# Fused cross-covariance attention and gated FFN on one core: the short chunk of v first in each batch, and the early loads in another order

## The chip, the cores and the metric

The kernel runs on one core of a Trainium2 chip. The metric is the device time of one execution in microseconds (us); smaller is better. Kernels that are compared ran in alternating rounds on the same chip. In the profile lines, PE is TensorE's products, PEld its weight loads, DVE VectorE, ACT ScalarE, POOL GpSimd and SPq SyncE's queue; a timeline line gives start and length in us, and in brackets the idle time before it and what ended it.

## The reference, cut to what matters

```python
# four batches, N = 6016 tokens, C = 256 channels, d_ff = 1536
qn = q / (norm(q, axis=1) + 1e-06);  kn = k / (norm(k, axis=1) + 1e-06)   # over the tokens
s = kn.transpose(0, 2, 1) @ qn / tau                  # 256 x 256 for each batch
a = softmax(s)
x = (v @ a).reshape(B * N, C)
out = (sigmoid(x @ w_gate) * (x @ w_val)) @ w_out
```

The matrix a of a batch needs all of that batch's q and k. After that, v can be streamed through in pieces. The kernel never forms x: it multiplies a into the weights first (G = a·w_gate, H = a·w_val), so that each piece of v needs only v·G, v·H and the output product.

## The kernel before

A batch has 47 tiles of 128 tokens, in chunks of four tiles and one "short" chunk of three. While TensorE streams the chunks of one batch, it also forms the scores of the next batch, and VectorE the squares for its norms. The work is laid out in slots: twelve slots a chunk, and slot f computes one slice of 128 of d_ff.

```python
groups = [(t, min(TPC, NT - t)) for t in range(0, NT, TPC)]     # TPC = 4, NT = 47: the short one is last
...
psg = pool("psg", 2, space=PSUM)     # gate products, two buffers
psv = pool("psv", 2, space=PSUM)     # value products, two buffers
...
def glu(b, ci, f):                   # one slot: 4 matmuls as wide as the chunk (512 or 384)
    ...
    nc.scalar.activation(out=g_sb[:, :n], in_=ps_gate[:, :n], func=ACT.Sigmoid)
    nc.vector.tensor_tensor(
        out=hts[b, ci][:, f, :n], in0=ps_val[:, :n], in1=g_sb[:, :n], op=ALU.mult)    # hT
...
for ci in range(NCH):                # the main loop, inside "for b in range(B)"
    for f in range(FC):              # FC = 12
        glu(b, ci, f)
        flush()                      # copies finished output rows out of PSUM, stores a finished chunk
        if prev is not None and not block:
            out_mms(*prev, f * TPC, (f + 1) * TPC)    # four output products of the chunk before
        for fn, a in side.get((ci, f), ()):           # loads, transposes, scores, squares
            fn(*a)
        if (b, ci) == (0, 0) and f < len(gh_order) - 5:
            gh(0, 5 + f, pso, "o")                    # the last 7 of batch 0's 12 pieces of G and H
```

The first two v chunks of batch 0 are transposed on TensorE, the others by a DMA that the SyncE queue issues. That queue works in order, and the store of a finished chunk stands in it ahead of the transpose of a later one.

## Time and profile before

| | before |
|---|---|
| median of the first three runs | 829.01 us (828.88 to 829.31) |
| the first profiled execution | 830.27 us, with a span of 828.2 us from first to last instruction |
| TensorE busy | 807.9 us, 98% of that span |
| VectorE, ScalarE busy | 590.2 us (71%), 392.2 us (47%) |

The prediction quotes the lines of this profile.

### The profile page before, as it was taken

Reading aid. Unit: us, or ns where it says so; the run is one execution under the profiler, and the core shown is the slowest. Engines: PE = TensorE matmul, PEld = TensorE weight load, DVE = VectorE, ACT = ScalarE, POOL = GpSimd, SP = SyncE. Lnnn points to the kernel's source line nnn. Section 1 sums busy time; section 2 is a strip of 40 time slices with the busy share of each in tenths; the row PEclk is TensorE's granted clock in tenths of the full one; section 3 lists DMA queues with packets and bytes.
Section 4 is the critical chain, followed back from the end, with each engine's and each line's share of the span. In section 5 each row is a group of like instructions: output and inputs, shape, how many; then the busy total and the mean of one; then the engine's idle time right before and its main releaser. Section 6 shows DMA issues by size and latency. Waiting matters only on the chain.

```text
span 828.2 us, 13621 instructions
## 1 busy us (share of the span) xinstructions
PE 807.9 (98%) x5122; PEld 499.1 (60%) x5134; DVE 590.2 (71%) x1025; ACT 392.2 (47%) x644; POOL 78.9 (10%) x151
## 2 busy tenths in 40 slices
PE   4799999999999999999999999999999999999998
PEld 2456666665665666665576666666566566666666
DVE  5777777887667777778767777777766666666665
ACT  3754444446644444445654444444655444444442
POOL 4432100002201100000221010000000000000000
PEclk9999999999999999999999999999999999999999
DMA  9999823226746443223875452223322323322211
GB/s 214 206 200 195 126 52 89 55 58 133 158 85 124 96 85 60 57 51 83 157 141 123 81 108 60 51 60 78 64 58 63 75 52 84 61 58 68 47 36 71
DMA packets 77874, 77.17 MB, mean 93 GB/s; under 512 B 50672, under 2 KB 55792, under 8 KB 77808
## 3 DMA queue, kind: packets, MB, share of 16 engines
q0 software_dynamic: 22768, 38.81, 28.5%
q1 hardware_dynamic: 54752, 36.91, 17.6%
q8 instruction: 40, 0.66, 0.3%
q10 hardware_dynamic: 288, 0.59, 0.2%
q14 instruction: 26, 0.21, 0.1%
HBM read 78.64 MB, written 24.64 MB: 125 GB/s over the span
## 4 chain that ended last, share of the span: by engine, by line
PE 92%; DMA 6%; DVE 1%; issue 0%; POOL 0%; ACT 0%; POOLq 0%
PE ps_o L88 29%; PE ps_gate L88 29%; PE ps_val L88 29%; PE ps_s L88 4%; DMA k_sb<-in_k_dram 3%; PE ps_gh L88 2%; DMA vT<-v_sb 2%; DMA w_gate<-in_moe_w_gate_dram 1%; DVE hT L434 0%; DVE sq L184 0%; PE ps_end L88 0%; ACT g_sb L433 0%; POOL q_sb L98 0%; PE ps_n L88 0%; POOL k_sb L98 0%
## 5 line engine op out<-in xcount | busy, mean ns | idle before, releaser
L434 DVE TENSOR_TENSOR hT<-ps_val,g_sb 128x512 bf16<-128x512 f32 (+1 forms) x576 | 391.0, 679 | 205.7 <-ACT g_sb L433 200.8
L433 ACT ACTIVATE g_sb<-ps_gate 128x512 bf16<-128x512 f32 (+1 forms) x576 | 338.2, 588 | 386.8 <-PE ps_gate L88 380.5
L88 PE MATMUL ps_gate<-vT,gh_G 128*128 128x512 bf16 (+1 forms) x1152 | 337.5, 375 | 0.7 <-DMA vT<-v_sb 0.5
L88 PE MATMUL ps_val<-vT,gh_H 128*128 128x512 bf16 (+1 forms) x1152 | 337.5, 375 | 0.3
L88 PE MATMUL ps_o<-w_out_sb,hT 128*128 128x256 bf16 x2244 | 324.9, 273 | 0.0
L88 PEld LDWEIGHTS <-hT 128*128 128x128 bf16 x2268 | 221.0, 98 | 124.7
L88 PEld LDWEIGHTS <-gh_H 128*128 128x128 bf16 x1152 | 112.7, 98 | 131.7 <-issue 1.0
L88 PEld LDWEIGHTS <-gh_G 128*128 128x128 bf16 x1152 | 112.4, 98 | 38.3 <-DMA vT<-v_sb 0.8
L460 DVE COPY out_sb<-ps_o 128x256 f32<-128x256 f32 x187 | 77.4, 414 | 12.6 <-PE ps_o L88 12.6
L88 PE MATMUL ps_s<-k_sb,q_sb 128*128 128x256 bf16 x376 | 71.2, 293 | 14.6 <-DMA k_sb<-in_k_dram 7.6
L108 POOL DMA_DIRECT2D v_sb<-in_v_dram x48 | 25.5, 532 | 601.3 <-DMA vT<-v_sb 452.0
L88 PEld LDWEIGHTS <-q_sb 128*128 128x128 bf16 x376 | 39.2, 105 | 23.7 <-issue 9.6
L223 DVE TENSOR_TENSOR acc<-acc,sq 128x1024 bf16<-128x1024 bf16 (+1 forms) x66 | 44.2, 669 | 0.0
L184 DVE TENSOR_TENSOR sq<-q_sb 128x1024 bf16<-128x1024 bf16 (+2 forms) x42 | 28.0, 666 | 1.2 <-DMA q_sb<-in_q_dram 1.1
L98 POOL DMA_DIRECT2D q_sb<-in_q_dram x44 | 24.2, 549 | 38.5 <-PE ps_s L88 12.4
L98 POOL DMA_DIRECT2D k_sb<-in_k_dram x44 | 24.0, 544 | 14.5 <-DMA k_sb<-in_k_dram 7.7
L184 DVE TENSOR_TENSOR sq<-k_sb 128x1024 bf16<-128x1024 bf16 (+2 forms) x34 | 22.4, 658 | 0.2 <-DMA k_sb<-in_k_dram 0.2
L182 ACT ACTIVATE sq<-k_sb 128x1024 bf16<-128x1024 bf16 (+1 forms) x11 | 10.7, 1010 | 12.0 <-DMA k_sb<-in_k_dram 8.9
L88 PEld LDWEIGHTS <-e_sb 128*128 128x128 bf16 x112 | 10.2, 98 | 6.0 <-issue 1.0
L88 PE MATMUL ps_gh<-w_val,e_sb 128*128 128x512 bf16 x45 | 13.5, 379 | 0.2
L88 PE MATMUL ps_gh<-w_gate,e_sb 128*128 128x512 bf16 x41 | 12.7, 379 | 1.0 <-DMA w_gate<-in_moe_w_gate_dram 0.8
L433 ACT ACT_TABLE_LOAD x6 | 7.7, 1283 | 9.0 <-PE ps_gate L88 9.0
(69 smaller groups left out, 123.2 us busy)
## 6 DMA issues: line engine op xcount, KB each, us to landing
out_dram<-out_sb SPq DMA_DIRECT2D x44, 512.0 KB, 2.9
v_sb<-in_v_dram POOLq DMA_DIRECT2D x44, 256.0 KB, 3.9
q_sb<-in_q_dram POOLq DMA_DIRECT2D x35, 256.0 KB, 6.5
k_sb<-in_k_dram POOLq DMA_DIRECT2D x35, 256.0 KB, 7.7
q_sb<-in_q_dram POOLq DMA_DIRECT2D x4, 512.0 KB, 11.5
k_sb<-in_k_dram POOLq DMA_DIRECT2D x4, 512.0 KB, 13.4
out_dram<-out_sb SPq DMA_DIRECT2D x3, 384.0 KB, 3.0
w_gate<-in_moe_w_gate_dram POOLq DMA_DIRECT2D x3, 256.0 KB, 8.0
```

Source lines behind the costliest of these rows:

```text
L88: nc.tensor.matmul(out, lhsT=lhsT, rhs=rhs, start=start, stop=stop, **kw)
L98: nc.gpsimd.dma_start(out=tl[:, :nt, :], in_=rows(src, b)[:, t0 : t0 + nt, :])
L108: nc.gpsimd.dma_start(out=v_sb[:, :nt, :], in_=rows(v, b)[:, t0 : t0 + nt, :])
L182: nc.scalar.activation(out=sq[:, :nt, :], in_=src[:, :nt, :], func=ACT.Square)
L184: engine.tensor_tensor(out=sq[:, :nt, :], in0=src[:, :nt, :], in1=src[:, :nt, :], op=ALU.mult)
L223: nc.vector.tensor_tensor(out=acc[:, :nt, :], in0=acc[:, :nt, :], in1=st[b]["sq", w][:, :nt, :], op=ALU.add)
L433: nc.scalar.activation(out=g_sb[:, :n], in_=ps_gate[:, :n], func=ACT.Sigmoid)
L434: nc.vector.tensor_tensor(out=hts[b, ci][:, f, :n], in0=ps_val[:, :n], in1=g_sb[:, :n], op=ALU.mult)
L460: nc.vector.tensor_copy(out=out_sb[:, s, :], in_=ps)
```

## The change

It has three parts. The short chunk comes first in each batch, so that the first piece of v is smaller and the stream can start earlier. During batch 0, the loads of the next batch's q and k are put eight slots later in program order (12 instead of 20 slots before use). And the output weights are loaded ahead of the third v chunk.

```diff
+    short = NT - (NCH - 1) * TPC
+    chunks = [(0, short)] + [(short + t * TPC, TPC) for t in range(NCH - 1)]
 ...
     def load_v(b, ci):
-        t0, nt = groups[ci]
+        t0, nt = chunks[ci]
 ... (the same in transpose_v, glu, out_mms, flush, last_rows and the last loop)
-            if lb < B:
-                at(ci * FC + 0, load_v, lb, lci)
             if (b, ci) == (0, 0):
                 at(0, load_w_out)
+            if lb < B:
+                at(ci * FC + (1 if (b, ci) == (0, 0) else 0), load_v, lb, lci)
 ...
-            at(max(0, s0 - 20), load_qk, n, t0, nt)
+            at(max(0, s0 - (12 if b == 0 else 20)), load_qk, n, t0, nt)
```

More of the change, by code (lines that the diff above doesn't have):

```diff
@@ L394, in transpose_v @@
     def transpose_v(b, ci, ps=None, late=None):
-        t0, nt = groups[ci]
+        t0, nt = chunks[ci]
         v_sb = vs.pop((b, ci))
@@ L414, in glu @@
     def glu(b, ci, f):
-        t0, nt = groups[ci]
+        t0, nt = chunks[ci]
         n = nt * P
@@ L440, in out_mms @@
     def out_mms(b, ci, n0, n1):
-        t0, nt = groups[ci]
+        t0, nt = chunks[ci]
         hT = hts[b, ci]
@@ L458, in flush @@
             out_sb, s, ps, b, ci = pending.pop(0)
-            t0, nt = groups[ci]
+            t0, nt = chunks[ci]
             nc.vector.tensor_copy(out=out_sb[:, s, :], in_=ps)
@@ L464, in last_rows @@
     def last_rows(b, ci):
-        t0, nt = groups[ci]
+        t0, nt = chunks[ci]
         s, half = nt - 1, C // 2
@@ L617 @@
             prev = (b, ci)
-    for s in range(groups[NCH - 1][1] - 1):
+    for s in range(chunks[NCH - 1][1] - 1):
         out_mms(*prev, s * FC, (s + 1) * FC)
```

## The prediction

> **What bounds the kernel now.** I read the page first (busy times, the chain that ended last), then the groups by shape, the busy time in stretches of my choosing, TensorE's waits, and last the timeline around each wait. The page gives TensorE (PE) 98% busy and 92% of the chain:
>
> ```profile
> PE 807.9 (98%) x5122; PEld 499.1 (60%) x5134; DVE 590.2 (71%) x1025; ACT 392.2 (47%) x644; POOL 78.9 (10%) x151
> PE 92%; DMA 6%; DVE 1%; issue 0%; POOL 0%; ACT 0%; POOLq 0%
> ```
>
> Busy is not proof, because matmuls overlap, so I measured from start to start in the timeline. Two 512-wide matmuls take 0.432 us (0.216 each), two 384-wide ones 0.324 (0.162 each), four 256-wide output products 0.436 (0.109 each). Against that spacing I looked for lost time. In stretches (each row: the stretch, its length, then busy time and count of PE, PEld, DVE, ACT, POOL, then granted clock, DMA share, GB/s):
>
> ```profile
> 4.00:39.00 35.00, 23.19 (x154) 15.33 (x157) 24.76 (x47) 18.94 (x23) 14.54 (x25) 1.00 1.12 215
> 39.00:53.00 14.00, 13.95 (x71) 6.49 (x71) 10.80 (x17) 10.48 (x18) 4.75 (x9) 1.00 1.24 205
> 72.00:88.00 16.00, 15.48 (x100) 9.59 (x99) 12.51 (x22) 6.55 (x11) 1.06 (x2) 1.00 0.99 146
> 88.00:820.40 732.40, 731.66 (x4629) 451.87 (x4636) 525.93 (x910) 346.51 (x579) 49.34 (x93) 1.00 0.39 81
> ```
>
> The reader is to see that only the first 39 us, at full DMA rate, leave PE much room; one wait of about half a microsecond lies before 88; and in the 732 us after that almost nothing is left. PE's waits name them:
>
> ```profile
> PE ps_s L88 <- DMA k_sb<-in_k_dram: 7.6, 6, 2.0
> PE ps_gh L88 <- DMA w_gate<-in_moe_w_gate_dram: 0.8, 2, 0.5
> PE ps_gate L88 <- DMA vT<-v_sb: 0.5, 1, 0.5
> ```
>
> The vT wait is one event, at the start of the fourth chunk (number 3, counting from 0) of the first batch. From the last output product's start at about 86.85 to 87.64 there are 0.79 us instead of 0.11: 0.68 us lost.
>
> ```profile
> 87.64 0.60 PE L88 MATMUL ps_gate<-vT,gh_G 128*128 128x512 bf16 x2 [0.52 <-DMA vT<-v_sb]
> 72.62 2.08 SPq L401 DMA_TRANSPOSE vT<-v_sb  x1
> ```
>
> Its DMA transpose was issued at 72.62, behind the output store of chunk 0 on the same queue, and landed 15.0 us later. Summed, the waits inside the stream after 39.0 that I can find are 0.68 (this one), 0.30 and 0.30 (near 254.8 and 454.3): some 1.3 us of 829. There is no more than this, plus the start, to win.
>
> **What the Trainium skill says.** "Perfetto Trace Analysis", section Identifying the Most-Contended Engine, warns that matmul busy time is a poor measure of the distance to the bound; hence the start-to-start spacing. "TensorE: Matmul & The Clock Gate", section Back-to-back issue gap, gives a warm gap of N/2.4 + 2.5 ns: 216, 162.5 and 109 ns for N = 512, 384 and 256. The trace agrees to the nanosecond (0.216, 0.162, 0.109), so matmul time here goes with columns, and moving columns between chunks is free. The page's lower sustained 131 ns for N = 512 isn't seen. "ScalarE: Activation LUTs", section What ACT_TABLE_LOAD costs, gives about 1283 ns a load (the trace: 1.28 us at 39.23, the first sigmoid at 40.52) and 186 + 0.833 N ns an activation: 506 at N = 384 and 613 at 512, measured 487 and 597. So a quarter fewer columns saves a sixth of ScalarE's time, not a quarter. "DMA: Bandwidth & Descriptors", section Queues, rings and completion order, says that engines alternate between queues packet by packet. That fits a transpose of small packets taking 15.0 and 16.1 us while the loads keep DMA full, against a median of 3.7 over the run.
>
> **The change part by part.** TensorE's total of columns doesn't change; the 3-tile chunk only changes its place in each batch.
>
> *Short chunk first, the start.* The first v load falls from 256 to 192 KB. At 1.25 us per 256 KB (successive landings in the trace) that is 0.31 us, and all six weight loads queue behind it. PE's last waits before the first gate product (0.54 at 36.19, 0.26 at 38.57) are for those weights, so the first gate product moves from 39.00 to 38.69: **-0.31 us**.
>
> *Short chunk first, chunk 0.* It now has 48 matmuls of 0.162 instead of 0.216, 2.59 us less PE work (given back in chunk 11). In a slot without output products PE then needs 4 x 0.162 = 0.648 us. Per slot the other engines' work shrinks less. The latency of one slot, from the last short chunk:
>
> ```profile
> 819.03 0.49 PE L88 MATMUL ps_val<-vT,gh_H 128*128 128x384 bf16 x2
> 819.23 0.49 ACT L433 ACTIVATE g_sb<-ps_gate 128x384 bf16<-128x384 f32 x1 [0.60 <-DVE hT L434]
> 819.75 0.56 DVE L434 TENSOR_TENSOR hT<-ps_val,g_sb 128x384 bf16<-128x384 f32 x1 [0.20 <-ACT g_sb L433]
> ```
>
> From the value product's start to the end of hT are 820.31 - 819.03 = 1.28 us, and about 0.06 passes until PE sees it. There are two PSUM buffers, so two slots take no less than 1.34 us, against PE's 2 x 0.648 = 1.296: 0.05 per two slots, 0.1 over slots 7 to 11. In slot 8 the PE transposes of chunk 1 are copied out by VectorE (0.42) and ScalarE (0.58), which that latency cannot hold: 0.1 to 0.2. At the front, ScalarE's table load still stands (39.23 before, 38.9 by my count now), and PE arrives 0.2 to 0.3 us earlier than before at products that need sigmoid 0, hT 0 and the copy of G and H behind it: 0.2 to 0.4 lost. Sum of chunk 0: **+0.5 us**. Its length: 12 x 0.648 + 7 pairs of G and H products at 0.432 + 8 transposes at 0.056 = 11.25 (the same sum with 0.864 gives 13.84; the timeline has 13.92, 39.00 to 52.92), plus 0.5: chunk 1 starts near 50.4.
>
> *Short chunk first, chunk 1 and after.* The short chunk's 36 output products fill nine slots of the next chunk, so the last three slots there have four products alone (0.864 us) while VectorE has hT (about 0.63 start to start) and squares for the next batch (0.68). Before, that fell in chunk 0 of batches 1 to 3 and cost 0.30 in batches 1 and 2:
>
> ```profile
> 252.57 0.69 DVE L434 TENSOR_TENSOR hT<-ps_val,g_sb 128x512 bf16<-128x512 f32 x1 [0.83 <-ACT g_sb L433]
> 253.50 0.68 DVE L184 TENSOR_TENSOR sq<-q_sb 128x1024 bf16<-128x1024 bf16 x1
> 254.84 0.59 PE L88 MATMUL ps_val<-vT,gh_H 128*128 128x512 bf16 x2
> ```
>
> Now it falls in chunk 1 of all four; batch 3 has no squares, batches 1 and 2 keep theirs, and batch 0 gets a new one: **+0.30 us**.
>
> *The vT wait.* Chunk 0's store now follows output product 36, not 48, three slots earlier, and chunk 0 is shorter: I put the issue of chunk 3's transpose near 65.5. With 15 to 16 us it lands near 81, and PE reaches chunk 3 near 83 (66.0, below, and a full chunk with its scores of 17). The wait goes: **-0.68 us**.
>
> *Weights of the output ahead of the third v chunk.* 768 KB took 3.95 us. v chunk 2 lands near 48.6 instead of 44.9, its transpose 16.1 us later near 64.7. PE reaches chunk 2 near 50.4 + 12 x 0.864 + 36 x 0.109 + 6 scores x 0.218 = 66.0 (69.8 before). One microsecond of margin for something that varies by as much: **+0.1 us** as an expected value. The output weights themselves land at 47.3, three microseconds before use.
>
> *Loads eight slots later.* GpSimd's queue waits for buffers[...], not for slots, and ran far ahead of PE before. Only its order changes (q and k of two groups now pass behind v, and v chunk 3 ahead of group 2): **0**, apart from its part in the two vT estimates. Scores of group 0 need data at about 53; it lands near 51.1.
>
> *The end.* Three tiles instead of two are stored by the next to last transfer, 128 KB more just before the final halves: **+0.1 us**.
>
> Sum: -0.31 + 0.5 + 0.30 - 0.68 + 0.1 + 0.1 = 0.0. So 829.01 stays 829.0.
>
> **Rivals.** (1) *It wins about a microsecond:* the vT wait and the head start count in full and the front of chunk 0 doesn't stall, because VectorE's part shrinks too. For it: DVE has only 10.80 us of work in the 14 us of chunk 0. Then 828.0. (2) *A new vT wait at chunk 2:* the transpose now lands behind PE, because its v chunk gave way to the weights. For it: 16.1 us in the same DMA jam before; against it: PE itself gets later by the stalls of chunk 0. It would cost 0.5 to 2 us: 829.5 to 831. (3) *VectorE becomes the bound in all short chunks:* in batches 1 and 2 the short chunk now meets the squares. Against it: PE needs 0.648 + 0.436 and a score there, about 1.2 us a slot, VectorE about 1.0. It would add up to 0.5 us for each of two batches: 830.
>
> **Range and chances.** Rival 1 sets the low end with a little for an unforeseen gain, 827.7; rival 2 in its middle the high end, 830.4. A change of 2% would be 16.6 us; all waits after the start make 1.3 us and the stream of matmuls is unchanged, so faster by 2% is out of reach, and slower by 2% needs a stall that recurs in every chunk: 0.005 each, within 2% 0.99.
>
> **What would show it.** Right: the first gate product near 38.7; no PE wait on vT at chunk 3; gaps of 0.1 to 0.4 in chunk 0 put down to VectorE or ScalarE; one new 0.3 us gap at the end of chunk 1 of batch 0, the other two moved by a chunk; the chain still over 90% PE, and PE's busy total within 2 us of 807.9. Wrong: a PE wait on vT of over half a microsecond, a wait of the scores on q or k after the start, or gaps recurring in later short chunks.

## The result, and the profile after

The changed kernel took 829.83 us (829.71 to 830.32, six runs), the kernel before 829.12 us (828.88 to 829.34, six runs). The ratio is 1.001, with a 95% interval of 0.9997 to 1.0023: the same. Still, each of the six runs of the changed kernel lay above all six of the kernel before: a small loss, which the interval can't tell from none.

The page of the changed kernel, its busy times and its chain by engine:

```profile
PE 806.3 (97%) x5120; PEld 498.2 (60%) x5132; DVE 589.7 (71%) x1025; ACT 392.0 (47%) x644; POOL 79.0 (10%) x151
...
PE 93%; DMA 3%; DVE 1%; ACT 1%; issue 0%; POOL 0%; POOLq 0%; ACTq 0%
```

Less DMA stands in the chain (3% against 6%) and nothing else moved much. Among TensorE's waits, the one on w_gate fell from 0.8 to 0.2 us and the one on vT is gone. A new one of 0.2 us has come, of a value product on gh_H, a piece of H (experiment 4 comes back to it). By these two profiles the changed kernel even had the shorter span: 827.9 us against 828.2. The timed runs said the opposite by 0.7 us, so both kernels were profiled again side by side.

### The profile page after: what moved, and what is told of

Same layout as the page of the kernel before. It is cut to its first block, busy times and chain, and to the rows that moved or that the text cites. A ratio compares the mean times of both kernels' runs of the same rounds, so it can differ in the third digit from the quotient of the medians.

```text
span 827.9 us, 13618 instructions
## 1 busy us (share of the span) xinstructions
PE 806.3 (97%) x5120; PEld 498.2 (60%) x5132; DVE 589.7 (71%) x1025; ACT 392.0 (47%) x644; POOL 79.0 (10%) x151
## 4 chain that ended last, share of the span: by engine, by line
PE 93%; DMA 3%; DVE 1%; ACT 1%; issue 0%; POOL 0%; POOLq 0%; ACTq 0%
PE ps_o L91 30%; PE ps_val L91 29%; PE ps_gate L91 29%; PE ps_s L91 4%; DMA k_sb<-in_k_dram 3%; PE ps_gh L91 2%; DVE hT L437 1%; ACT g_sb L436 0%; DVE sq L187 0%; PE ps_n L91 0%; POOL q_sb L101 0%; PE ps_end L91 0%; ACT L545 0%; POOL k_sb L101 0%; DVE gh_G L392 0%
## 5 line engine op out<-in xcount | busy, mean ns | idle before, releaser
L91 PEld LDWEIGHTS <-q_sb 128*128 128x128 bf16 x376 | 38.5, 103 | 24.7 <-issue 10.3
L436 ACT ACT_TABLE_LOAD x6 | 7.7, 1283 | 9.4 <-PE ps_gate L91 9.3
```

The lines of the kernel that those rows point to most:

```text
L91: nc.tensor.matmul(out, lhsT=lhsT, rhs=rhs, start=start, stop=stop, **kw)
```

## The experiments

The stalls below are read from the timeline as in the prediction: from start to start, less what the matmuls between take (0.216, 0.162 and 0.109 us for widths 512, 384 and 256).

### 1. Both kernels again, unchanged

There is no edit. For the kernel before:

> The kernel before, unchanged, run again beside the others, to see how its profile varies. The first profile of it came from an execution of 830.27 us, which is 1.2 us over the median of its timed runs. If that profile is typical, the wait on vT at chunk 3 (0.68 us) and the first gate product at 39.0 come again, and the changed kernel should then be 0.3 us faster, as the two profiled spans say. If it was an outlier, this one shows a shorter wait on vT or an earlier first gate product, by about 1 us in sum, and a span near 827.2.

For the changed kernel:

> The changed kernel, unchanged, on the same chip as its parts. Expected as on record: ratio 1.000 to 1.002 (829.1 to 830.5 us), first gate product near 38.3, no wait on vT at chunk 3, stalls of 0.27, 0.35 and 0.20 us in chunk 0 and 0.30 us at the end of chunks 1 of batches 0, 1 and 2.

Measured in the same rounds: the kernel before 829.42 us (828.92 to 829.49) with a span of 827.2, the changed kernel 829.96 us (829.83 to 830.14) with a span of 827.9. Nine further runs of the kernel before gave 829.39 us. Ratio of the changed kernel 1.0008 (0.9995 to 1.0020); of the kernel before to itself 1.0001. Here too each run of the changed kernel lay above all fourteen of the kernel before.

The first profile was not typical: of the 38 timed runs of the kernel before, the slowest took 830.08 us, less than its 830.27. TensorE's waits in the second profile of the kernel before:

```profile
PE ps_s L88 <- DMA k_sb<-in_k_dram: 7.7, 6, 2.0
PE ps_s L88 <- ACT k_sb L136: 7.2, 1, 7.2
PE ps_r L88 <- ACT e_sb L324: 0.4, 1, 0.4
PE ps_gh L88 <- DMA w_gate<-in_moe_w_gate_dram: 0.3, 1, 0.3
```

The wait on vT, 0.5 us in the first profile, isn't there, and the wait on w_gate is 0.3 us instead of 0.8. In the timeline, the DMA transpose was issued at almost the same time as in the first profile, and the first product of chunk 3 follows without a wait:

```profile
72.26 2.29 SPq L401 DMA_TRANSPOSE vT<-v_sb  x1
...
86.59 0.59 PE L88 MATMUL ps_gate<-vT,gh_G 128*128 128x512 bf16 x2
```

The view of this tile gives the transpose's time to landing, which was 15.0 us in the first profile:

```profile
DMA to landing us min/median/max: 12.8/12.8/12.8
```

It landed at 85.1, and TensorE needed it at 86.59: 1.5 us to spare. In the first profile it came 0.7 us too late.

Now the chunks of batch 0, in two stretches of both second profiles (columns as in the prediction). First the kernel before, then the changed one:

```profile
38.50:53.00 14.50, 14.50 (x75) 6.65 (x74) 10.99 (x18) 10.97 (x18) 4.75 (x9) 1.00 1.24 205
...
90.00:819.70 729.70, 729.43 (x4622) 450.28 (x4620) 523.99 (x907) 345.90 (x577) 47.73 (x90) 1.00 0.39 80
```

```profile
38.50:53.00 14.50, 14.28 (x86) 7.79 (x85) 10.62 (x19) 10.51 (x20) 5.11 (x10) 1.00 1.23 206
...
90.00:819.70 729.70, 729.43 (x4608) 448.89 (x4606) 523.82 (x904) 345.79 (x575) 47.75 (x90) 1.00 0.39 80
```

In the long stretch TensorE is busy 729.43 us in both. In chunk 0 it is busy all of 14.50 us before and has holes after. Busy time shows too little of them, as matmuls overlap; the timeline of the changed kernel shows them in full:

```profile
40.60 0.49 PE L91 MATMUL ps_gate<-vT,gh_G 128*128 128x384 bf16 x2
41.05 0.48 PE L91 MATMUL ps_val<-vT,gh_H 128*128 128x384 bf16 x2
41.54 0.59 PE L91 MATMUL ps_gh<-w_val,e_sb 128*128 128x512 bf16 x2
...
47.27 0.33 PE L91 MATMUL ps_val<-vT,gh_H 128*128 128x384 bf16 x1
47.78 0.34 PE L91 MATMUL ps_val<-vT,gh_H 128*128 128x384 bf16 x1 [0.19 <-DVE gh_H L392]
...
49.70 0.49 PE L91 MATMUL ps_gate<-vT,gh_G 128*128 128x384 bf16 x2
50.23 0.48 PE L91 MATMUL ps_val<-vT,gh_H 128*128 128x384 bf16 x2
50.55 0.59 PE L91 MATMUL ps_gate<-vT,gh_G 128*128 128x512 bf16 x2
```

A pair of 384-wide products should take 0.324 us. From 40.60 to 41.05 there are 0.45, from 41.05 to 41.54 0.49, from 49.70 to 50.23 0.53. A single one should take 0.162 and takes 0.51 from 47.27 to 47.78. In sum some 0.84 us are lost. The last line is the first product of chunk 1: chunk 0 took 50.55 - 38.43 = 12.12 us against a calculated 11.25, so 0.87 lost in all. In the kernel before it took 52.55 - 38.64 = 13.91 against 13.84: 0.07.

And the end of chunk 1 of batch 0, where the short chunk's output products have run out. The stall itself falls on the first value product of chunk 2, at 66.88:

```profile
66.15 0.59 PE L91 MATMUL ps_gate<-vT,gh_G 128*128 128x512 bf16 x2
66.88 0.59 PE L91 MATMUL ps_val<-vT,gh_H 128*128 128x512 bf16 x2
67.31 0.60 PE L91 MATMUL ps_o<-w_out_sb,hT 128*128 128x256 bf16 x4
```

From 66.15 to 66.88 there are 0.73 us instead of 0.432: 0.30 lost. The same stall stands at 267.7 and 467.1. The kernel before has it twice, near 253.8 and 453.3.

So the balance between the two second profiles is: first gate product 38.43 instead of 38.64, -0.21; chunk 0, 0.87 - 0.07 = +0.80; chunk 1 of batch 0, +0.30. That makes +0.89 by chunk 3. Chunk 3 begins at 83.57 and at 86.59; the moved matmuls are 48 x 0.054 + 12 x 0.109 = 3.90 us, the difference is 3.02, which is 0.88 short, as summed. From there to TensorE's end the changed kernel takes 3.80 us more instead of 3.90, so 0.10 comes back. The sum of +0.78 fits the spans of these two profiles (827.9 - 827.2 = 0.7) and the medians of the first rounds (+0.71); the medians of these rounds give less (+0.54). The second profile of the kernel before is no average either: it shows the fastest of the five runs, 828.92 us. Over all five runs of each kernel in these rounds, the median spans are 827.4 and 827.9.

### 2. The short chunk alone, and the loads alone

The short chunk first, with the loads of before (the edit is to the changed kernel):

```diff
-            if (b, ci) == (0, 0):
-                at(0, load_w_out)
             if lb < B:
-                at(ci * FC + (1 if (b, ci) == (0, 0) else 0), load_v, lb, lci)
+                at(ci * FC + 0, load_v, lb, lci)
+            if (b, ci) == (0, 0):
+                at(0, load_w_out)
-            at(max(0, s0 - (12 if b == 0 else 20)), load_qk, n, t0, nt)
+            at(max(0, s0 - 20), load_qk, n, t0, nt)
```

> The short chunk first, but loads and output weights in the order of before. Theory (the short chunk does both the good and the bad, the order of loads does nothing): within 0.3 us of the whole change, the same stalls in chunk 0 and chunk 1, and no wait on vT at chunk 3, as its transpose is issued near 66. Rival (the reordered loads are what took the vT wait away): the wait at chunk 3 is still there, 0.5 us or more, and the time is 0.5 us over the whole change.

Measured, in the rounds of experiment 1: 829.99 us (829.78 to 830.26), ratio 1.0008 (0.9995 to 1.0020), span 828.0. That is the whole change's 829.96 and its ratio. The stalls late in chunk 0 (0.36 and 0.20) and at the end of chunk 1 (0.30) have the sizes that they have in the whole change, and there is no wait on vT.

The loads alone (the reverse edit, on the kernel before):

> The two changes of load order alone, chunks as before. Theory: 829.0, no change: the vT wait at chunk 3 stays at 0.5 to 0.9 us, because its transpose still stands behind the store of chunk 0 near 72. Rival: fewer loads ahead of it, so the transpose lands sooner and the wait goes: 0.7 us faster than before. A third outcome would be that v chunk 2, now behind the output weights, delays its own transpose past the start of chunk 2 near 69.8: not expected, as it should land near 64.

Measured, in the same rounds: 829.13 us (829.11 to 829.38), ratio 0.9998 (0.9986 to 1.0011), span 827.1. As expected nothing changed in the time. The expected wait on vT wasn't there, as experiment 1 by now explains. But the rival was right about the transpose. Issued at 72.23, it took, by the view of its tile:

```profile
DMA to landing us min/median/max: 8.4/8.4/8.4
```

So it landed at 80.7, 5.9 us ahead of its use, against 1.5 in the kernel before. With the short chunk first, the same comparison gives landings of 83.1 without the new loads and 80.4 with them, for uses at 83.63 and 83.57: 0.5 and 3.2 us ahead. These are single profiles, and the two of the kernel before differ by 2.5 us between themselves. But both pairs point the same way, and three more profiles with the short chunk first and the new loads (the first one and the two of experiment 4) give landings of 80.5 to 81.0. So the loads' new order seems to buy margin against a wait that was seen in one execution, not time in a typical one.

### 3. The stall at the end of chunk 1: output products three to a slot

```diff
+    def rows_of(prev):
+        return chunks[prev[1]][1]
 ...
-                    out_mms(*prev, f * TPC, (f + 1) * TPC)
+                    out_mms(*prev, f * rows_of(prev), (f + 1) * rows_of(prev))
```

> The changed kernel with the short chunk's 36 output products spread three to a slot over the next chunk's twelve slots, instead of four to a slot over nine. Theory: the 0.30 us stall at the end of chunk 1 in batches 0, 1 and 2 comes from three slots without output products, where TensorE asks for hT faster than VectorE gives it; with 0.33 us of output products in every slot it goes, so 0.9 us less than the changed kernel (about 829.0). Rival: VectorE's order (hT behind a square) stalls TensorE in those slots whatever stands between, and nothing changes. Side effect to look at: the store of chunk 0 and the transpose of v chunk 3 behind it come about 3 us later, near 69, so that transpose may land at or past the start of chunk 3 (83.6) and give back 0 to 1 us as a wait on vT.

Measured: 829.38 us (828.85 to 829.41), span 827.0. The kernel before took 829.57 us (829.22 to 829.74) in these rounds; ratio 0.9997 (0.9984 to 1.0009). The profiled span fell by 0.9 us from the 827.9 of the changed kernel. But it is that of the fastest of five runs; the other four have 827.4, and the kernel before has a median of 827.5 in these rounds. The place of the stall at 66.15 in experiment 1 now reads:

```profile
66.05 0.59 PE L91 MATMUL ps_gate<-vT,gh_G 128*128 128x512 bf16 x2
66.48 0.59 PE L91 MATMUL ps_val<-vT,gh_H 128*128 128x512 bf16 x2
66.91 0.60 PE L91 MATMUL ps_o<-w_out_sb,hT 128*128 128x256 bf16 x4
```

These are 0.43 us apart, and the two later stalls are gone as well. So spreading the products removes the stall, and the rival is refuted: hT still stands behind a square (64.13, hT at 64.73) and TensorE doesn't wait. Which of the edit's two effects does it is not shown. It makes the last three slots of the chunk longer, and it also moves a copy on VectorE. In the changed kernel the short chunk's last output row is copied in just the slot of the square (VectorE, experiment 1):

```profile
65.21 0.41 DVE L463 COPY out_sb<-ps_o 128x256 f32<-128x256 f32 x1
65.54 0.68 DVE L187 TENSOR_TENSOR sq<-q_sb 128x1024 bf16<-128x1024 bf16 x1
66.14 1.28 DVE L437 TENSOR_TENSOR hT<-ps_val,g_sb 128x512 bf16<-128x512 f32 x2
```

By the code's two buffers, the value product at 66.88 needs the first of these two hT, which ends near 66.83. The copy holds VectorE for 0.33 us, as much as the stall of 0.30; after the edit it comes at 67.93. Moving it alone might have been enough, and no run tried that. The copy alone isn't enough for the stall: batch 3, which has the copy in that place but no squares, has none. The side effect, a wait on vT, didn't come: the transpose was issued at 68.85, landed 11.2 us later at 80.1, and chunk 3 began at 83.18.

With the transpose of v chunk 3 also put ahead of the store:

```diff
-                at(ci * FC + 2, transpose_v, nb, nci)
+                at(20 if (nb, nci) == (0, 3) else ci * FC + 2, transpose_v, nb, nci)
```

> As after_spread, with the transpose of v chunk 3 issued before the store of chunk 0 (slot 20 instead of 26). It waits only for its v, which lands near 55, so it should be issued near 55 and land near 70, 13 us ahead of need. Theory: 0.9 us below the changed kernel, no wait on vT at chunk 3; if after_spread shows a wait there, this one is faster than it by that wait, else equal to it within 0.2 us.

Measured: 829.31 us (828.92 to 829.52), ratio 0.9997 (0.9984 to 1.0009), span 826.9: equal, as there was no wait to take away. The transpose was issued at 55.20, as expected, but took 19.7 us in the full DMA queues, not the 15 that I had assumed; it landed at 74.9, 8 us ahead of use.

### 4. Two stalls of chunk 0, one at a time

ScalarE's table load earlier:

```diff
     nc.scalar.copy(*late.pop())
+    nc.scalar.preload_act_table(ACT.Sigmoid)
     gh_tiles(0)
 ...
-    gh(0, 3, psv, "v", act=True)
-    nc.scalar.preload_act_table(ACT.Sigmoid)
+    gh(0, 3, psv, "v", act=False)
```

> The changed kernel with ScalarE's table load for the sigmoid put ahead of its copies of G and H (into a stretch in which it waits 1 us), and the fourth of these copies given to VectorE. Theory: the stall of 0.27 us near 41 (0.13 and 0.16 in the second profile) is set by that table load (38.69 to 39.97), the first sigmoid then ends by 39.5 and the stall goes: 0.2 to 0.3 us less. Rival: the stall is set by VectorE's copies of G and H between the hT, then it stays or grows, as VectorE has one more.

Measured, in the rounds of experiment 3: 829.81 us (829.77 to 829.95), ratio 1.0004 (0.9991 to 1.0016), span 827.8. ScalarE's timeline, and TensorE's where the stall was:

```profile
36.40 1.28 ACT L538 ACT_TABLE_LOAD   x1
37.69 0.69 ACT L390 ACTIVATE gh_G<-ps_gh,rrow 128x512 bf16<-128x512 f32 x1
39.02 0.49 ACT L436 ACTIVATE g_sb<-ps_gate 128x384 bf16<-128x384 f32 x1 [0.64 <-PE ps_gate L91]
...
40.65 0.49 PE L91 MATMUL ps_gate<-vT,gh_G 128*128 128x384 bf16 x2
40.98 0.49 PE L91 MATMUL ps_val<-vT,gh_H 128*128 128x384 bf16 x2
41.30 0.59 PE L91 MATMUL ps_gh<-w_val,e_sb 128*128 128x512 bf16 x2
```

In experiment 1 the table load stood at 38.62 and the first sigmoid began at 39.92, right behind it. Now the first sigmoid waits for TensorE, not for its table, and the products are 0.33 and 0.32 us apart. The stall is gone although VectorE has one copy more, so ScalarE's work ahead of the first sigmoid set it. The edit moves both the table load and one copy of 0.69 us out of that place; their shares weren't measured apart. The time shows little: the span fell by only 0.1 us, because the first gate product came at 38.49 in this execution. From there to chunk 3 (83.34) are 44.85 us, against 83.57 - 38.43 = 45.14 before the edit: 0.29 less.

The last copy of G and H on ScalarE:

```diff
-                    gh(0, 5 + f, pso, "o")
+                    gh(0, 5 + f, pso, "o", act=True if f == 6 else None)
```

> The changed kernel with the last of the twelve G and H copies of batch 0 (slot 6 of chunk 0) on ScalarE instead of VectorE. Theory: the 0.35 us stall near 47.7 comes from hT of slot 6 standing behind that 0.74 us copy on VectorE; it goes, while ScalarE has 0.69 more in a slot of 1.08 and may give back 0.1 us. The 0.20 us stall near 50.2 (the copies of the transposes) stays. So 0.25 to 0.35 us less. Rival: with 0.65 us a slot and two buffers the chain through ScalarE and VectorE is too long in any case, and the stall only moves to the next slots.

Measured, in the same rounds: 829.67 us (829.41 to 830.28), ratio 1.0004 (0.9990 to 1.0017), span 827.6. The place where 0.35 us were lost:

```profile
46.92 0.49 PE L91 MATMUL ps_gate<-vT,gh_G 128*128 128x384 bf16 x2
47.25 0.49 PE L91 MATMUL ps_val<-vT,gh_H 128*128 128x384 bf16 x2
47.57 0.61 PE L407 MATMUL ps_tp<-ident_bf,v_sb 128*128 128x128 bf16 x8
```

It has no gap, and from the first gate product to chunk 3 are 83.19 - 38.39 = 44.80 us, 0.34 less than the 45.14; the stall at the copies of the transposes (0.20) stays, and so does the first one. So that one copy was the cause, but not as expected, by holding up hT. In the trace of experiment 1 TensorE waits for the copy itself:

```profile
46.99 0.74 DVE L392 TENSOR_SCALAR gh_H<-ps_gh,rrow 128x512 bf16<-128x512 f32 x1
47.64 0.55 DVE L437 TENSOR_TENSOR hT<-ps_val,g_sb 128x384 bf16<-128x384 f32 x1
47.78 0.10 PEld L91 LDWEIGHTS <-gh_H 128*128 128x128 bf16 x1 [0.58 <-DVE gh_H L392]
```

The copy writes the last piece of H, and the value product of slot 8 is the first to use it, as weights. The copy ends at 47.73, and the weight load and the stalled product start at 47.78; the hT behind the copy ends only at 48.19, too late to have released them. In the second profile of the kernel before, the same copy ends at 49.23, just in time for its use at 49.29. In both edits the saving is below what the timed runs resolve.

### 5. All repairs together, on both orders of chunks

The four edits of experiments 3 and 4 on the changed kernel:

> The changed kernel with the four repairs together: output products three to a slot after a short chunk, the transpose of v chunk 3 ahead of the store, the sigmoid's table load early, the last G and H copy on ScalarE. If the stalls are separate terms, they add: 0.90 + 0.27 + 0.35 us come off the changed kernel's span of 827.9, leaving 826.4, some 0.8 us below the kernel before (ratio 0.999). Of chunk 0's stalls only the 0.20 us at the copies of the transposes stays. Rival: ScalarE, which now has the table load earlier and one copy more, opens a new stall in chunk 0 that takes back half of it.

And the full chunk first, as in the kernel before, with the changed kernel's loads and the two edits of experiment 3 (`rows_of` taken from `groups`):

> The full chunk first as in the kernel before, with the new order of loads, the transpose of v chunk 3 ahead of the store, and output products three to a slot after a short chunk. Chunk 0 has no stall here, the 0.30 us stalls of batches 1 and 2 go: 0.6 us below the kernel before, a span near 826.6. Together with the other run it says what the short chunk first is worth by itself once its stalls are repaired: its earlier start (0.2 us) less the 0.2 us left at the transposes, so equal within 0.3 us.

| in the same rounds | median us (range) | ratio to before (95%) | span us | expected span |
|---|---|---|---|---|
| before | 829.03 (828.86 to 830.08) | | | |
| short chunk first, all repairs | 828.39 (827.99 to 828.58) | 0.9989 (0.9976 to 1.0001) | 826.3 | 826.4 |
| full chunk first, loads and two repairs | 828.60 (828.41 to 828.65) | 0.9991 (0.9978 to 1.0005) | 826.7 | 826.6 |

Both spans came out within 0.1 us, as do the medians of the five spans of each (826.3 and 826.6), so the stalls are separate terms and add up. In the first, only the 0.20 at 49.45 us of chunk 0 is left; in the second, chunk 0 loses 0.08 in all (13.92 against 13.84). All five runs of each lie below all nine of the kernel before, yet the intervals just include 1: by the measure used here these are still "the same" time. The short chunk first, once repaired, is worth 0.2 us by the medians, with ranges that overlap.

## Why the prediction was right or wrong

The time was right as forecast: the same within 2%, inside the range, 0.8 us above the centre. The chief reason held: TensorE's stream is unchanged, and there were only tenths of a microsecond to win or lose. With all waits at 1.3 us against the 16.6 of 2%, that forecast could hardly fail; the sum is the test. But the sum of 0.0 came out as about +0.8 between like profiles, and this is where.

- **The vT wait, -0.68: this step failed.** The wait existed in one profile and was taken for typical. A second profile of the same kernel has no such wait, and the transpose lands 1.5 us early. The text had the warning at hand, in the execution's 830.27 us against a median of 829.01, and yet it took the wait of the one off the time of the other. Whether the occasional slower runs of the kernel before (830.08 is the slowest timed) have that wait isn't known: timed runs of it have no traces here.
- **The start, -0.31: right in mechanism.** In the paired profiles it was -0.21. Over all the profiles the first gate product came at 38.6 to 39.0 with a full first chunk (four profiles) and at 38.2 to 38.5 with the short one (eight); the means are 0.4 apart.
- **Chunk 0, +0.5: right in mechanism, too small.** It lost 0.80 more than before. The front measured 0.29 in the middle of its 0.2 to 0.4, and experiment 4 showed ScalarE's work ahead of the first sigmoid to be its cause: the table load, or the copy that the same edit moved, or both. The 0.20 at the copies of the transposes is also as given. The term that was left out is 0.35: VectorE copies the last piece of H in slot 6, the value product of slot 8 needs it, and slots 7 and 8 are now 0.65 us each, so TensorE gets there before the copy has ended. For these slots the prediction looked at the way from value product to hT and at the copies of the transposes, not at this need. The 0.1 from the bare latency of two buffers wasn't seen; slots without an extra operation run at 0.65 us.
- **Chunk 1 of batch 0, +0.30: right**, and in batches 1 and 2 the stall moved by one chunk at the same size. The account of it was incomplete: beside hT and the square it left out the copy of an output row, 0.33 us of VectorE's time in the same slot. Experiment 3 removed the stall but doesn't separate this copy from the missing output products.
- **Output weights first, +0.1: it cost nothing.** The transpose of v chunk 2 landed at 63.8 (48.36 and 15.5 us), for a use at 66.15. So rival 2 didn't come.
- **Loads later, 0: right for the time.** That nothing but vT estimates hangs on it fits as well: experiment 2 saw the transpose of chunk 3 land 2.7 to 4.4 us earlier, unseen in the time.
- **The end, +0.1: not seen.** After TensorE's last product come 827.9 - 824.7 = 3.2 us in one kernel and 827.2 - 824.0 = 3.2 in the other.
- **Rival 3** didn't come: the short chunks of batches 1 to 3 have no new stall. Rival 1's argument, 10.80 us of VectorE's work in 14 us, was about an average; the stalls came from single operations in single slots.

The whole loss, then, belongs to the short chunk first; experiment 2 shows that it alone gives the same time, and the loads alone give none.

## What to carry to other kernels

When only tenths of a microsecond are left, ask whether the profiled execution is typical before building on any wait in it: compare its own time with the timed runs, or profile the same kernel twice. Making a piece of work smaller for the engine that bounds can shrink its slots more than the work of the engines behind it (here TensorE's slot from 0.864 to 0.648 us, a sigmoid from 0.597 to 0.487, a copy of G or H not at all), and a single copy that a long slot hid then stalls the stream. Look for these slot by slot, not in averages; spreading filler work evenly, and moving one-time operations such as a table load into an idle stretch, removed most of them.

## What the Trainium skill lacked or had wrong

- "TensorE: Matmul & The Clock Gate", section Back-to-back issue gap: it calls 131 ns the sustained spacing at N = 512, and N/2.4 + 2.5 only the isolated one. In this kernel's sustained stream, with a weight load for each matmul, the spacing was 0.216 us at 512, 0.162 at 384 and 0.109 at 256 for hundreds of microseconds: the formula's values. 131 ns was never seen.
- "ScalarE: Activation LUTs", section What ACT_TABLE_LOAD costs: besides 1283 ns it counts a drain of about 1380 ns for each switch. The load took 1.28 us here, the copy before it ended at 36.38, and the next activation began right after (load at 36.40, activation at 37.69). No such second part was seen.
- "DMA: Bandwidth & Descriptors", section DMA Transpose (X-bar): it doesn't say how long a transpose takes beside loads that fill the queues. The same transpose of 256 KB (v chunk 3 of batch 0) took from 8.4 to 20.0 us here, against a median of 3.7 over the first profile, and 12.8 and 15.0 us in two executions of the same kernel.
- No page gives how far one profiled execution of a kernel may lie from its timed ones: here 830.27 against a median of 829.01 us, more than the whole change.
